# Another order of work in a polysketch attention and mixture-of-experts attention kernel

## The chip, the cores and the metric

The kernel runs on one core of a Trainium2 chip. The metric is the time of one execution on the device in microseconds (us). The engines are named as in the profile: PE (TensorE, matmuls; PEld its weight loads), DVE (VectorE), ACT (ScalarE), POOL (GpSimd) and SP (SyncE, which issues most of the DMAs). Each engine carries out its own instructions in the order in which the program issues them, and waits on semaphores for what other engines and DMAs have to deliver.

## The reference

A linear attention over four batches of four heads is followed by an attention of four experts, of which each row of the sequence uses two.

```python
def phi(x):                       # q, k, v: (4, 4, 1088, 32); S1, S2: (8, 32)
    a = np.einsum('rd,bhsd->bhsr', S1, x)
    b = np.einsum('rd,bhsd->bhsr', S2, x)
    return np.einsum('bhsi,bhsj->bhsij', a, b).reshape(*x.shape[:-1], 64)
q_p, k_p = phi(q), phi(k)
kv  = np.einsum('bhsf,bhsd->bhfd', k_p, v)
num = np.einsum('bhsf,bhfd->bhsd', q_p, kv)
den = np.einsum('bhsf,bhf->bhs', q_p, k_p.sum(2))[..., None] + 1e-06
x = (num / den).transpose(0, 2, 1, 3).reshape(4, 1088, 128)

topk, w = ...                     # the 2 best of 4 logits x @ w_gate, softmax over the 2
for e in range(4):
    q, k, v = x @ wq[e], x @ wk[e], x @ wv[e]          # 128 -> 64
    a = causal_softmax(q @ k.T / 8)
    ye = a @ v @ wo[e]
    for kk in range(2):
        out += (topk[:, :, kk] == e)[..., None] * w[:, :, kk:kk+1] * ye
```

The output has the shape (4, 1088, 128), in f32.

## The kernel before

**Work and tiles.** The loop over the four batches (batch, L1285) writes down the same jobs for each. First the polysketch attention: k, q and v are loaded by halves or quarters and turned by DVE; PE makes the two sketches of each (job "sketch", L524); DVE turns them back ("back", L527); DVE or POOL multiplies them into 64 features ("features", L529 to L532); PE sums the features with v ("sums") and divides for x. Batch 0 does it by rows (attend_rows, L603), the batches 1 to 3 turned (attend_turned, L696), which are prepared while the batch ahead of them runs its experts. Then choose_experts (L811) makes the gate: logits on PE, some twenty small DVE instructions, and masks that go through DRAM.

The experts' attention works on 17 tiles of 64 rows a batch; as each row has two chosen experts a tile fills 128 partitions. The tiles come in three groups, (0,6), (6,12) and (12,17) (L141). For each group queries (L1011) makes the queries of all experts and picks the chosen ones with a predicated copy (L1031). For each tile scores (L1045) makes a chain over all engines: score on PE (L1056), take with mask and maximum on DVE (L1068), exp on ACT (L1084), guard on ACT or POOL (L1090, L1092), invert on DVE (L1095), weigh on POOL (L1099), turn A on DVE (L1104). values (L1114) then multiplies with x on PE (L1132), sorts the sums by expert (L1162 to L1175: keep, patch, spread and scale V), and outputs (L1201) projects with the folded weights Mo, copies out of PSUM and stores. The last group of the last batch has its own end (L1219 to L1242): three pieces of 128 rows, each with a copy "keep out 3.0.x" by ACT or DVE (L1238) and a store "store out 3.0.x" by SP or ACT (L1241).

**The order of the work.** Nothing is scheduled by the compiler. job (L78) only notes a job: its name, the engine or the two engines that can do it, what it reads and makes, and the buffers that it holds. The list ORDER (L22) then names all 1287 jobs by number, and Plan.run (L84) issues them in this order. A letter behind a number picks the engine: a is the first of the job's two, b the second; for a dummy b means that it is left out. A job's figures of time, landing and rank in the code were used in making the list and do nothing in the kernel. Buffers are handed out from queues of free ones in the order of the list, so the list also sets which earlier job a buffer's next user waits for. PSUM has four pairs of banks (the pool "ps"), SBUF has three query buffers "qs", three of masks "mb", six of working tiles "w", two of each of "AT", "agg" and "ob".

```python
n, a = (int(word[:-1]), "ab".index(word[-1])) if word[-1] in "ab" else (int(word), 0)
j = self.jobs[n]
if j["eng"][a] != "-":
    for h in j["holds"]:
        if h not in self.where:
            self.where[h] = free[h[0]].popleft()
    j["f"](j["eng"][a])
```

**The jobs that the text speaks of**, by their numbers. 2 and 3: loads of S1 and S2, by SP and ACT. 4: "table" (L247), a first activation, with which ACT loads its table. 5 to 44: dummies (L250), each of two matmuls of 128x512 in bf16 on a buffer of zeros; the result isn't used. 52: load of the weights w0 by SP. 60 and 63: pick8 and onehot, small constants. 74 and 75: load k0.0 by SP and k0.1 by ACT (L429). 76 and 77: load q0.0 by SP and q0.1 by ACT. 78 to 81: loads of v0 by SP. 95: features k0.2, by POOL or DVE. 106: keep sums 0.0 and 109: keep qf 0.0, copies out of PSUM by ACT or DVE (L194 is the one copy helper). 177 and 219: reciprocals of the gate's shares (L906). 402 and 403: turn k1.0 and k1.1 on DVE (L490). 406 to 408: sketch k1 and its two back transposes. 385: out 0.2, the projection of batch 0's last group (L1210). 557 and 558: score and take of tile 1.7. 1126 and 1130: scale V 3.0.x, by POOL or DVE. 1135, 1137, 1139: keep out 3.0.0, 3.0.1 and 3.0.2; 1136, 1138, 1140: their stores.

Of the kernel before, what the change touches and what calls it, by code (L numbers as in the profile page):

```python
# [27 lines left out]
205 173 430 223 245 189 249a 166a 190a 693 699 250a 421 215 436 206 207 431 211a 194 216 318 195 432a 691 212 251 319  # L28
217 160 433a 134 322a 434 161a 247 196 213 248 224 29b 252 698 703 437 197a 438a 191 214 439a 690 704 192 267 268 706a
705 225a 420 323a 193 198 218a 199 219 422 269 324 220 695a 275 276 71 145 320 73 709a 696a 72 277 440 137 423 321 990  # L30
325 278 221 291 270 200 260 707a 279a 226 292 141 708a 261 293 711a 177 262 710a 263a 280 271a 441 443b 227 283 228 442a
284 178a 281 34b 285 272 286 282 253 991 713 461 294 136 326 327 712 462 254 714a 255 229 264 702 287a 273 265 328 256a
230 231 295b 463 465 994 715 464 716 296 30b 989 144 11b 288 140 266 274 701 721 466 289 329 330b 138 233a 722a 297 335
290 257 358 235b 234a 232a 237 258 236 331 298 334 43b 359 361 351 467 350 31b 360 336 471 362 363 238 342 337 352 239
343 723 476 344 338b 332 259 477 468 345 353 346b 478 725 472 354a 724 333 479 444 364b 139 347 339 18b 28b 299 300 480b
448 301 302 365 726 340 481b 482 447 303 304 305a 341 483 348 445 306a 719 349 307b 366 519 241 240 985 520 308a 505 446
473 474 143 310 309 732 242 367 311 987 512 506 355 142 733 243a 312 543 14b 986 356 513 727 491 514 542 734 357 498 521
515b 492 314 507 717 315 499 735a 313 544 469 728 316a 522b 36b 41b 545 730b 736a 5b 516 500 501b 368 737 718 523 546a
493 997 475a 547b 548 369 244 370 452 371 494a 549 372 373 517 374 729b 375 376 377a 450 524 996 502 525 484 731 518 495
988 508b 378b 380b 588 589 485 509 720 15b 503 381 455 379a 486 382 35b 487b 510 550 496 590 591 511 384 497 738 504 551  # L40
565 592a 453 740a 739a 564 566 572 573 488 383 580 489 574 490 581 992a 451 582 1000 575 758 460 576a 44b 449 454 1002
616 577 615 1004b 552 1001 993b 567 759 760 470 618 619a 617 1008b 620a 593 594 761 526 527 528 12b 553a 621 622 1003a
578 37b 554 529a 530a 1007a 555 568b 579 531a 534 385 33b 1005b 763 583 639 1006a 532a 569 386 584a 570 640 533 623 456
764 317 585 571 648 457 556 557 586 535 641 624 595 647 536 642 558 765 1010 458 649 762 625 587 1009 632 559 560b 631
774 655 650 16b 626 627a 561 633 773 562 656 1011a 651a 995 634 538 776 652 628 653 563 657 635b 778a 658 629 777b 779
636 388 659 643b 775 780 539 537 644 768 1012 637 802 630 803 660 795 796 540a 769 654 661a 816 817 797 645 1018 596 770
597 662 646 19b 663 1013 1019b 598 781 39b 818 664 788 599 771 804 459 805b 782 600 789 601 638 806 798a 783 741 790 389
999 742 799 998 665 604a 603b 744 666 602a 606 605a 667 745 607 668 743 772a 1020 609 746 608 766 387 1022 38b 669 784b
1021 670 785 23b 786 840 787 809 26b 751 1023 1024 839 791a 1029 1030 807 843b 844a 671 1025 1017 672 1027a 810 673 792
819b 676a 675a 800 845 677a 841 811 541 1031 674b 679 749 842 820 846 1032a 40b 611 610 755 678 808 1026a 1028 747 1033a  # L50
847 612 821 812a 1016 21b 862 848 1014 1034 748 801 1015 681 813 885 680 861 613a 886 822 887 849 814 1035 793 863 854
767 1036b 794 877 878 815 850a 855 24b 869 879 870 888 913 912 864 865b 1037a 916a 753 856 866 871 1055 823 857a 757 824
917b 1056 825 858 867 918 915 851 1057 880 872 914 889b 1058 890 390 881b 827a 882 682 883 873a 831 1059 874 919 884
1060 891 859 826a 830 868 828a 860 952 953 852 683 754 853 936 833 27b 937 929 928 829a 875 954 955 892 938 930 956 920
921 957 832 944 931 1065 939 922 945 1061 750 958b 940b 1063 1141 1144 946 1142 959 1143 923 876 893 960 941 1146a 1066
947 894 614 1038 924b 756 942 1145b 948b 925 1147 895 752 896 897 949 898 943 961 1067 1148 899a 687 902a 901b 835 932a
900a 1042 904 926 20b 1039 903 950 834 1172 1171 1041 905 933 1040 836 1149 1156 951 837a 1173 906 1068 1150 1188 934
927 1187 1180 1174 1175b 935 1189 1157 1179 1163 1190 684 1164 1215 1165 1158 686 1069a 13b 1166 1181 1151 1217 1214
1167b 1182 1216 1159b 1176 962 1219b 1218b 1064 963 964 1168 1177 965 1183a 966 1045 838 1191a 1220 1221 1169 967 968
1152a 1178 1153 1160 1184 969 970 971a 974a 1170 1222 1192 973b 975 1185 1193 1194 1223 1246 972a 976 977 1247 1257 1255  # L60
1048 1154 1224 1225 1248 1186 1254 6b 978 1256 1071 1070 1161 1162 1231 1258 1044 1249 1062 1230 1232 1075a 1226b 685
1250b 1155 1227 1239 1228 1238 1050 907 1047 1074b 1259 1046 1076 1072 1260b 1233 908 1251 1234b 1073 909 1252 979 1240
1077 1241 910a 1235 1043 1106 1261 1229 1236 1085 1242b 980 1262 1107 1086 1049 1237 1108 1109a 1253 911 1099 1243 1051
1110 1113 1195 1111 1114 982 1196 1053 1263 984 1100 1087 981 1197 1115 1198 1101 1078 1088b 1244 1245 1092 1054 983
1116a 1199 1200 1079 1089 1093 1102a 1094 1264 1052 1090 1201a 1265 1266 1267 1268 1202a 1095b 1204b 1206 1080 1269
1081a 1270 1203b 1207 1205 1091 1271 1096 1082 1272 1097 1083 1208 1103 1084 1211 1104 1117 1118 1276a 1210 1098 1119
# [1283 lines left out]
```

## Time and profile before

| | us |
|---|---|
| runs | 264.88, 262.51, 262.26 |
| their median | 262.51 |
| the profiled execution | 260.8 |
| its span, from its first to its last record | 259.0 |
| busy in it: PE, DVE, POOL, ACT | 249.3, 210.4, 158.4, 105.3 |
| granted clock of PE, mean | 0.997 |

The profile is of one execution, and its times count from the span's start. A row of a timeline gives the start, the duration, the engine, the line, the operation with its tiles (out<-in, partitions x elements, type) and how many instructions the row takes together (x); in square brackets, where the engine was idle before it, how long, and what it waited for. "ACTq" and "SPq" are the queues in which ACT and SP issue DMAs. "L1132" is line 1132 of the kernel.

### The profile page before, as it was taken

Reading aid. Unit: us, or ns where it says so; the run is one execution under the profiler, and the core shown is the slowest. Engines: PE = TensorE matmul, PEld = TensorE weight load, DVE = VectorE, ACT = ScalarE, POOL = GpSimd, SP = SyncE. Lnnn points to the kernel's source line nnn. Section 1 sums busy time; section 2 is a strip of 40 time slices with the busy share of each in tenths; the row PEclk is TensorE's granted clock in tenths of the full one; section 3 lists DMA queues with packets and bytes.
Section 4 is the critical chain, followed back from the end, with each engine's and each line's share of the span. In section 5 each row is a group of like instructions: output and inputs, shape, how many; then the busy total and the mean of one; then the engine's idle time right before and its main releaser. Section 6 shows DMA issues by size and latency. Waiting matters only on the chain.

```text
span 259.0 us, 9930 instructions
## 1 busy us (share of the span) xinstructions
PE 249.3 (96%) x4158; PEld 185.1 (71%) x4159; DVE 210.4 (81%) x532; ACT 105.3 (41%) x276; POOL 158.4 (61%) x271
## 2 busy tenths in 40 slices
PE   8798988999999999999999999999999999999994
PEld 3477554566498896665789786765896975789984
DVE  6998999999988787989998389899979649794342
ACT  2354446762704407634643034623525317243220
POOL 4867589948488816196762798283683633733640
PEclk9999999999999999999999999999999999999998
DMA  6953489505359445304403671404442226440012
GB/s 217 239 147 94 133 231 202 114 11 112 121 82 254 119 127 144 109 3 112 112 3 47 135 215 58 134 3 146 107 66 76 61 66 184 121 110 3 3 34 56
DMA packets 40381, 27.88 MB, mean 108 GB/s; under 512 B 25872, under 2 KB 35600, under 8 KB 40336
## 3 DMA queue, kind: packets, MB, share of 16 engines
q1 hardware_dynamic: 39744, 26.56, 42.0%
q8 instruction: 32, 0.52, 0.9%
q10 hardware_dynamic: 592, 0.69, 0.7%
q14 instruction: 13, 0.11, 0.2%
HBM read 22.62 MB, written 4.62 MB: 105 GB/s over the span
## 4 chain that ended last, share of the span: by engine, by line
PE 83%; POOL 7%; DVE 4%; DMA 3%; issue 2%; ACTq 1%; ACT 0%; SPq 0%; POOLq 0%; DVEq 0%
PE pair L1132 30%; PE pair L1056 26%; PE pair L1018 9%; PE pair L1260 7%; POOL fp L532 4%; PE pair L1210 3%; DMA in<-in_k_dram 2%; PE pair L771 2%; PE pair L576 1%; PE pair L524 1%; PE pair L1236 1%; DVE w L527 1%; PE pair L822 1%; POOL w L548 1%; DMA md<-cT 1%
## 5 line engine op out<-in xcount | busy, mean ns | idle before, releaser
L1099 POOL TENSOR_SCALAR w<-w,rs,sh 128x192 f32<-128x192 f32 (+14 forms) x68 | 55.9, 827 | 32.9 <-DVE rs L1095 31.4
L1056 PE MATMUL pair<-xT,qs 128*128 128x384 f32 (+11 forms) x216 | 73.6, 478 | 1.9 <-DVE rs L1095 1.0
L1084 ACT ACTIVATE w<-w,mx 128x192 f32<-128x192 f32 (+16 forms) x68 | 52.5, 773 | 50.1 <-DVE mx L1068 44.8
L1056 PEld LDWEIGHTS pair<-xT,qs 128*128 128x128 f32 x216 | 38.3, 190 | 28.5 <-issue 11.9
L1104 DVE STREAM_TRANSPOSE AT<-w 128x128 f32<-128x128 f32 (+14 forms) x68 | 50.7, 759 | 6.2 <-POOL w L1099 6.0
L1068 DVE CUSTOM_DVE_ANT_0 w<-pair,mask 128x896 f32<-128x896 f32 (+15 forms) x68 | 48.2, 724 | 4.4 <-PE pair L1056 3.5
L1166 POOL TENSOR_TENSOR agg<-agg,mb 128x768 f32<-128x768 f32 (+1 forms) x22 | 34.0, 1560 | 18.6 <-issue 8.7
L1132 PEld LDWEIGHTS pair<-AT,xra 32*128 32x128 f32 x1136 | 41.6, 185 | 3.7 <-DVE AT L1104 1.1
L1132 PE MATMUL pair<-AT,xra 32*128 32x160 f32 (+5 forms) x1136 | 44.1, 302 | 0.0
L194 ACT COPY agg<-pair 128x384 f32<-128x384 f32 (+1 forms) x36 | 15.0, 467 | 52.3 <-PE pair L1132 47.8
L1018 PE MATMUL pair<-xT,Mq 128*128 128x384 f32 (+1 forms) x96 | 34.3, 479 | 0.0
L532 POOL TENSOR_TENSOR fp<-w 128x576 f32<-128x576 f32 x22 | 27.1, 1250 | 1.3 <-DVE w L527 0.6
L1132 PE MATMUL pair<-AT,xrb 32*128 32x160 f32 (+5 forms) x752 | 27.3, 287 | 0.0
L1132 PEld LDWEIGHTS pair<-AT,xrb 32*128 32x128 f32 x752 | 26.4, 185 | 0.8 <-issue 0.7
L1031 DVE COPY_PREDICATED qs<-mb,pair 128x768 f32<-128x768 uint16 (+1 forms) x24 | 23.2, 967 | 1.8 <-DMA mb<-me 0.8
L1018 PEld LDWEIGHTS pair<-xT,Mq 128*128 128x128 f32 x96 | 17.0, 190 | 9.5 <-DVE mx L1068 1.1
L1092 POOL TENSOR_SCALAR rs<-zs 128x1 f32<-128x1 f32 x34 | 8.2, 242 | 23.8 <-ACT w L1084 21.9
L1260 PEld LDWEIGHTS pair<-Mo,agg 128*128 128x128 f32 x168 | 20.6, 192 | 2.7 <-issue 0.8
L1260 PE MATMUL pair<-Mo,agg 128*128 128x128 f32 x168 | 21.1, 276 | 0.0
L527 DVE STREAM_TRANSPOSE w<-pair 128x576 f32<-128x576 f32 x16 | 11.8, 760 | 3.9 <-PE pair L524 3.7
L194 DVE COPY agg<-pair 128x384 f32<-128x384 f32 (+1 forms) x10 | 5.1, 523 | 11.5 <-ACT agg L194 10.6
L1162 DVE COPY_PREDICATED agg<-mb,pair 128x384 f32<-128x384 uint16 (+1 forms) x24 | 12.6, 548 | 2.0 <-ACT agg L194 2.0
(173 smaller groups left out, 290.4 us busy)
## 6 DMA issues: line engine op xcount, KB each, us to landing
xra<-xd SPq DMA_DIRECT2D x16, 192.0 KB, 3.9
xrb<-xd SPq DMA_DIRECT2D x16, 192.0 KB, 4.7
xrc<-xd SPq DMA_DIRECT2D x16, 160.0 KB, 3.9
in<-in_k_dram SPq DMA_DIRECT2D x7, 272.0 KB, 4.3
mb<-me SPq DMA_DIRECT2D x3, 576.0 KB, 4.2
mb<-me SPq DMA_DIRECT2D x6, 288.0 KB, 5.6
in<-in_q_dram SPq DMA_DIRECT2D x3, 544.0 KB, 5.2
xd<-w SPq DMA_DIRECT2D x12, 136.0 KB, 3.6
```

What stands on the lines that cost most here:

```text
L194: (nc.scalar.copy if eng == "ACT" else VEC[eng].tensor_copy)(o, i)
L532: VEC[e].tensor_tensor(out=f, in0=a[:, :, None, R : 2 * R].to_broadcast([128, NJ, R, R]), in1=a[:, :, 0:R, None].to_broadcast([128, NJ, R, ...
L1018: nc.tensor.matmul(plan[ps[x]][:, y, 0:w], Mq[:, ((1, 2), (0, 3))[x][y]], plan[xT][:, 64 * t0 : 64 * t1], start=True, stop=True)
L1031: nc.vector.copy_predicated(chosen(), c, rows(plan[ps[x]]))
L1056: nc.tensor.matmul(plan[p][:, y, 0 : c1 - c0], plan[qs][:, 128 * t : 128 * t + 128], plan[xT][:, c0:c1], start=True, stop=True)
L1068: nc.vector.tensor_tensor_reduce(out=o, in0=src, in1=msk, scale=-1.0, scalar=mx[:, b, i, x - 1 : x] if x else 3e38, op0=ALU.add, op1=ALU.m ...
L1084: nc.scalar.activation(out=a, in_=a, func=ACTF.Exp, bias=mx[:, b, i, last : last + 1], scale=-1.0, accum_out=zs[:, b, i : i + 1])
L1099: nc.gpsimd.tensor_scalar(out=a, in0=a, scalar1=rs[:, b, i : i + 1], scalar2=plan[("sh", b)][:, i : i + 1], op0=ALU.mult, op1=ALU.mult)
L1104: nc.vector.transpose(dst[:, 0 : keys // 32, t], plan[A][:, 0:keys].rearrange("p (j s) -> p j s", s=32))
L1132: nc.tensor.matmul(plan[Vk[g // 2]][:, g % 2, lo : 32 * nt], plan[(f"xr{j // 12}", b)][rows, j % 12], a[rows, j, lo:], start=(j == 0), sto ...
L1166: nc.gpsimd.tensor_tensor(out=a, in0=a, in1=masks_in(plan[mb], w)[:, 2 * x : 2 * x + 2], op=ALU.mult)
L1260: nc.tensor.matmul(plan[p][0:m, 0, 128 * x : 128 * x + 128], plan[agg][:, e, 128 * x : 128 * x + m], Mo[:, e], start=(e == 0), stop=(e == ...
```

## The change

Only the list ORDER is changed, in all of its lines. It names the same 1287 jobs; some 72 of them have another letter, and so another engine: among them copies out of PSUM (L194), about thirty guards (L1090, L1092), the features k0.2 (95), the scale V 3.0.x (1126, 1130). The dummy 13 (18) is carried out in the new list and left out in the old one, so eight dummies run in place of seven. The order within each engine differs nearly everywhere. At the start, ACT's table (4) is ahead of load k0.1 (75), and pick8 (60) is POOL's first piece of work. Out 0.2 (385) comes ahead of score and take 1.7.0 (557, 558) in the old list and behind them in the new one. At the end, keep out 3.0.1 (1137) is on DVE and its store (1138) on SP; in the old list both were ACT's.

The first lines of both lists, the lines with the jobs named above, and the last:

```diff
 ORDER = """
-400 1 0 22a 2 3 84 76 48 45 77 49 74 42a 46 9a 51 88 10a 75 52 4 85 50 89 17a 86 87 78 81 401 47 97 90 98 79 100a 80 7a
-54 58 53 397 66 59 99 64 25a 391 82a 102a 65 56 92 395 91 392 101b 83a 103b 394 67a 95b 110 96a 60 94a 93a 403 111a 396
-402 112 114 115a 113a 108 109b 105 57 104 107b 106b 406 116 63a 122 399a 408 407 117a 126 55 398a 118 68 123 70 127 69
-61 128 124 410a 119 393 413a 414b 62a 692 133 409a 120 129a 411a 121b 405 416 412a 125a 415 404 697 146 417a 148 147 154
-130 149 152 162 163 179 418 180 150 132 424 153 184a 155 156 425a 151 689 183a 131 158 169 174 182 157a 167 159a 168 688
-181 170 185 426 164 694 171 186 700 427 201 208 419 202 135 175 428 176 203 187 222 204a 209 188 172 429 246 435 165 210
...
-325 278 221 291 270 200 260 707a 279a 226 292 141 708a 261 293 711a 177 262 710a 263a 280 271a 441 443b 227 283 228 442a
...
-578 37b 554 529a 530a 1007a 555 568b 579 531a 534 385 33b 1005b 763 583 639 1006a 532a 569 386 584a 570 640 533 623 456
...
-32b 1273a 1274a 1209 1112 1277 1275a 1105 1120 1278 1121 8b 1122 1212a 1128 1123a 1125 1280 1279 1213 1127a 1281 1124
-1126b 1131 1129 1132 1133 1282 1130b 1134 1135b 1284 1139a 1286 1285 1283 1140b 1136a 1137a 1138b
+1 3 0 2 48 76 77 4 74 51 37b 75 10a 60 46 52 84 50 81 54 49 88 8a 45 89 7a 17a 85 22a 78 80 97 86 79 53 87 400 98 100a
+397 90 55 99 91 92 63b 83a 64 391 102a 47 101b 96a 392 66 103b 24a 19a 59 82a 65 67a 401 114 115a 396 39b 108 95a 94a
+110 111a 93a 403 56 109a 112 113a 105 104 106a 394 116 58 402 406 107b 57 122 408 407 123 395 410a 117a 68 126 118 69
+413a 409a 127 119 399a 61 128 120 398a 393 70 414b 124 129a 412a 405 416 121b 125a 411a 62a 415 404 146 147 152 688 148
+154 417a 693 162 418 163 153 149 179 180 183a 155 150 424 425a 156 158 151 167 184a 131 168 181 157a 170 130 689 169
+159a 185 419 182 426 186 201 700 164 9b 174 215 175 427 133 202 208 132 165 428 203 209 176 216 204a 171 429 205 430 246
+222 245 166a 435 210 211a 223 436 217 187 206 694 172 431 207 433a 177 212 250a 691 194 432a 18a 249a 195 137 318 160
...
+569 453 621 768 579 1006a 528 529a 585 557 622 553a 530a 32b 531a 1005b 558 760 623 33b 593 624 317 625 586 533 761 385
...
+1104 1098 1105 982 1211 1278 1275b 1120 984 1121 1276a 1122 1123a 1277 1128 1279 1125 1280 1281 1126a 1212a 1127a 1213
+1124 1131 1132 1133 1129 1282 1284 1283 1130a 1134 1139a 1285 1135b 1286 1140b 1136a 1137b 1138a
 """.split()
```

More of the change, by code (lines that the diff above doesn't have):

```diff
@@ new lines @@
+413a 409a 127 119 399a 61 128 120 398a 393 70 414b 124 129a 412a 405 416 121b 125a 411a 62a 415 404 146 147 152 688 148
+154 417a 693 162 418 163 153 149 179 180 183a 155 150 424 425a 156 158 151 167 184a 131 168 181 157a 170 130 689 169
+159a 185 419 182 426 186 201 700 164 9b 174 215 175 427 133 202 208 132 165 428 203 209 176 216 204a 171 429 205 430 246
+222 245 166a 435 210 211a 223 436 217 187 206 694 172 431 207 433a 177 212 250a 691 194 432a 18a 249a 195 137 318 160
+173 218a 188 319 247 699 697 437 189 219 213 196 248 161a 251 690 438a 197a 434 252 439a 323a 322a 190a 703 421 422 191
@@ new lines @@
+224 192 692 220 268 214 704 420 705 193 423 706a 267 71 698 134 72 269 276 707a 275 440 710a 73 277 135 270 324 320 225b
+221 198 321 271b 708a 199 226 292 227 272 291 325 23b 278 695a 696a 293 200 178a 273 441 145 442a 31b 253 136 702 228
+274 283 711a 443a 254 701 294 279a 28b 284 709a 260 326 280 327 295a 261 285 461 296 462 262 712 255 328 329 713 281
+714a 229 230 330b 231 715 256a 297 263b 721 463 286 282 464 233b 466 235a 257 264 359 258 465 358 722a 471 716 298 140
+234a 351 265 360 232a 141 237 236 259 238 266 350 989 334 335 467 287a 139 352 720 985 472 361 138 342 343 239 362 16b
@@ new lines @@
+331 723 468 288 336 344 353 289 363 332 991 290 476 479 337 724 345 477 725 333 364a 354b 355 480a 481b 726 478 356 365
+299 14b 300 301 302 303 304 338a 482 483 143 241 346a 306a 366 339 340 732 990 444 142 367 448 307a 305a 718 341 473 347
+447 445 733 505 446 474 308b 240 242 348 309 311 310 727 512 986 728 506 519 243b 994 312 513 545 520 514 349 498 499
+515a 988 357 544 521 144 314 729a 491 516 996 313 38b 315 469 507 543 15b 542 734 992b 316a 546a 997 492 508b 475a 493
+735a 494a 20b 517 368 26b 522a 736a 369 509 370 495 500 993a 371 372 451 719 547b 501b 29b 548 523 717 373 524 510 374
@@ new lines @@
+375 518 450 449 737 376 730b 484 731 549 525 377a 496 379a 502 503 244 378b 497 380a 485 383 589 588 486 550 382 381 738
+452 511 11b 590 551 572 573 740a 564 574 384 487a 504 739a 565 488 575 576a 580 581 566 1000 489 582 758 615 490 591 577
+1002 1004b 616 470 583 618 759 552 459 617 567 1001 526 568a 619a 578 1008a 592a 620a 584b 527 987 25b 762 1007b 1003a
+569 453 621 768 579 1006a 528 529a 585 557 622 553a 530a 32b 531a 1005b 558 760 623 33b 593 624 317 625 586 533 761 385
+1010 534 570 559 386 763 594 1009 626 1011a 627a 536 769 764 532b 554 535 587 648 1012 647 571 560a 639 628 640 649 595
@@ new lines @@
+765 774 999 629 631 561 630 562 458 641 632 460 773 778a 656 642 655 455 555 776 775 633 538 657 770 777a 643a 1013 563
+634 995 650 658 644 779 651a 780 539 659 556 537 771 635b 540a 795 802 796 645 456 636 41b 387 652 653 660 454 1014 661a
+803 637 646 662 816 1018 596 663 654 597 817 1019b 598 599 998 664 781 457 638 788 782 789 818 600 601 741 790 665 772a
+804 819a 12b 602b 797 745 603b 744 791b 604a 820 541 792 605a 666 805b 607 821 742 608 806 667 606 1020 609 390 822 807
+668 783 1017 1021 1022 40b 743 669 388 1023 670 766 1024 27b 1029 751 839 809 810 840 784b 1025 671 672 1030 43b 673 747
@@ new lines @@
+785 1026a 844a 808 748 841 843a 1027a 1031 1028 793 675a 786 842 1016 811 787 798b 676a 845 812a 612 677a 1015 1033a
+1032a 749 846 389 13b 674a 794 756 813 678 679 611 799 800 854 885 1034 855 610 613a 750 35b 886 887 861 862 888 847 863
+848 814 681 864 1035 1037b 815 878 801 680 856 877 870 869 849 34b 754 889b 857a 746 879 850a 913 912 871 1036a 1055 823
+824 916b 872 1056 865b 1057 1058 890 851 1059 825 873a 6b 1065 917b 866 767 880 914 829a 1066 757 827a 915 918 752 858
+828a 867 826a 881b 868 859 682 852 891 919 882 929 1060 830 853 928 937 874 892 875 831 936 883 1061 945 683 833 930 884
@@ new lines @@
+931 938 832 920 876 932b 921 753 953 614 922 860 21b 944 946 952 939 1063 947 1142 923 954 1141 1067 955 933 948a 1146a
+1143 956 1144 893 949 1145a 686 1038 934 957 958a 894 940a 1039 1147 1148 959 960 895 935 896 897 898 901a 1172 1171 755
+924b 950 900a 925 961 1041 42b 941 951 904 834 899a 835 926 1164 1163 902a 44b 927 1173 905 903 1040 1187 1042 1165 1149
+1150 1188 1156 1189 36b 942 836 1190 906 1174 1191b 1215 943 1068 684 837b 1069a 687 1180 1151 1157 1158 1179 1192 1217
+1181 1214 1159b 1216 962 1064 1182 963 1219b 1183b 964 1152b 965 1166 1044 1175a 1193 838 966 1160 1153 1167b 967 1184
@@ new lines @@
+1218a 1161 1220 1194 968 1185 969 1221 970 1168 1176 1222 1162 685 972a 973a 976 1255 971b 974a 1045 1154 1254 977 975
+978 1177 1223 1155 1256 1257 1258 1230 1224 1178 1259 1047 1247 1225 1231 1246 1169 1071 1052 1046 1070 1248 1062 1186
+907 1260a 1073 5b 1051 1232 1226b 1075a 1072 1043 1261 1262 909 1048 1074b 1238 1227 1249 908 1170 1076 1228 1050 1233
+1077 1239 1106 1234a 910a 1240 1235 1229 1085 979 1236 1086 1107 911 1241 1250a 980 1242b 1251 1243 1108 1244 1245 1263
+1113 1099 1195 1109a 1049 1252 1196 1100 1114 30b 1197 1087 1088a 1253 1198 1237 1078 1092 1054 1093 1115 1094 1079 1199
@@ L69 @@
+1200 1201b 1095b 1264 1096 1080 1265 1205 1266 1267 1204b 1116b 1110 1081b 1268 1053 1089 1117 1269 1082 983 1083 1202b
+1090 1101 1203b 1111 1207 1091 1084 1270 1206 1208 981 1102a 1271 1103 1272 1118 1209 1112 1119 1210 1097 1273a 1274a
+1104 1098 1105 982 1211 1278 1275b 1120 984 1121 1276a 1122 1123a 1277 1128 1279 1125 1280 1281 1126a 1212a 1127a 1213
+1124 1131 1132 1133 1129 1282 1284 1283 1130a 1134 1139a 1285 1135b 1286 1140b 1136a 1137b 1138a
 """.split()
```

37 lines of the change are left out of this document (removed).

## The prediction

> **What bounds the kernel now.** I read the page first: busy time by engine, then the 40 slices, then the chain that ended last. The slices show where TensorE (PE) is not full, and the chain's shares show what it was waiting on there.
>
> ```profile
> PE 249.3 (96%) x4158; PEld 185.1 (71%) x4159; DVE 210.4 (81%) x532; ACT 105.3 (41%) x276; POOL 158.4 (61%) x271
> PE   8798988999999999999999999999999999999994
> PE 83%; POOL 7%; DVE 4%; DMA 3%; issue 2%; ACTq 1%; ACT 0%; SPq 0%; POOLq 0%; DVEq 0%
> ```
>
> PE is the bound: 96% busy and 83% of the chain. It is under 9 only in the first slices and in the last one. The second view is the table of windows, cut where PE first runs without gaps (42.12) and where DVE's last copy is nearly over (255.60). Columns: the stretch, its length, then busy us of PE, PEld, DVE, ACT and POOL with counts, PE's clock, the DMA share, GB/s.
>
> ```profile
> 0.00:42.12 42.12, 36.00 (x758) 22.45 (x759) 37.16 (x111) 19.39 (x54) 30.00 (x76) 1.00 0.71 178
> 42.12:255.60 213.48, 213.30 (x3400) 162.67 (x3400) 173.21 (x422) 85.41 (x221) 128.42 (x196) 1.00 0.39 94
> 255.60:259.00 3.40, 0.00 (x0) 0.00 (x0) 0.03 (x1) 0.53 (x2) 0.00 (x0) 0.80 0.28 71
> 5.40:15.40 10.00, 8.50 (x200) 5.93 (x202) 9.26 (x13) 3.92 (x7) 8.98 (x20) 1.00 1.03 226
> 26.00:42.10 16.10, 13.94 (x168) 7.74 (x164) 15.44 (x60) 8.96 (x31) 11.80 (x33) 1.00 0.76 184
> ```
>
> So the time has three parts. In 213.48 us PE is idle for 0.18: no order can shorten it while PE's work is the same, it can only put stalls in. In the first 42.12 PE is idle for 6.12 and part of its busy time is dummies; there DVE is the bound (9.26 of 10.00, 15.44 of 16.10). The tail of 3.40 has no PE at all. A new order can gain at the start and in the tail, and lose anywhere.
>
> The sum is made against the profiled run, 260.8 us: a span of 259.0 and 1.8 around it. The median of the runs is 262.51, 1.71 above; I add the sum's change to the median.
>
> **The change, part by part.** Both lists hold the same 1287 jobs. About 72 words take another engine. PE has one job more (an eighth dummy) and one change of mode fewer (68 to 67).
>
> *Tail.* Timeline of the last stretch (start, duration, engine, line, instruction, idle before and releaser):
>
> ```profile
> 253.38 0.52 DVE L1175 TENSOR_TENSOR agg<-agg,mb 128x384 f32<-128x384 f32 x1
> 253.49 1.82 SPq L1216 DMA_DIRECT2D out_dram<-ob  x4
> 255.34 0.29 DVE L194 COPY ob<-pair 128x128 f32<-128x128 f32 x1 [1.44 <-PE pair L1236]
> 255.61 0.27 ACT L194 COPY ob<-pair 128x128 f32<-128x128 f32 x1 [3.37 <-PE pair L1236]
> 255.66 0.36 SPq L1242 DMA_DIRECT2D out_dram<-ob  x1
> 256.30 0.27 ACT L194 COPY ob<-pair 128x128 f32<-128x128 f32 x1 [0.42 <-ACT ob L194]
> 256.60 0.35 ACTq L1242 DMA_DIRECT2D out_dram<-ob  x1
> ```
>
> ACT copies piece 2, issues its store, and only then copies piece 1 and issues that: last issue at 256.60. In the new list piece 1 is DVE's (1137b), right behind piece 0, and its store is SP's (1138a). DVE's copies end at 255.34+0.29 = 255.63 and about 255.63+0.29 = 255.92. The store goes out when copy and SP allow: the copy-to-issue gap is 0.03 (255.63 to 255.66), so 255.95 by the copy; SP's own pitch is 1.82/4 = 0.455, so 255.66+0.455 = 256.12 by the queue. That is 256.60-256.12 = 0.48 earlier; I take -0.5. The ends: 256.60-255.95 = -0.65, and 0 if SP's second store is held as long as ACT's was. The landing behind the last issue is 1.6 either way by the row below.
>
> ```profile
> out_dram<-ob ACTq DMA_DIRECT2D x2, 64.0 KB, 1.6
> ```
>
> *The load of k0.1.* On ACT's queue it stood ahead of the activation table (75 before 4); now it stands behind (4 before 75). Two views: ACT's timeline, and the DMA issues (KB each, then median us from issue to landing).
>
> ```profile
> 1.82 0.44 ACTq L429 DMA_DIRECT2D in<-in_k_dram  x1
> 2.29 1.28 ACT L247 ACT_TABLE_LOAD   x1 [2.29 <-issue]
> 3.59 0.20 ACT L247 ACTIVATE warm<-warm 128x1 f32<-128x1 f32 x1
> ```
>
> ```profile
> in<-in_q_dram SPq DMA_DIRECT2D x1, 272.0 KB, 3.3
> in<-in_q_dram ACTq DMA_DIRECT2D x1, 272.0 KB, 3.8
> in<-in_k_dram ACTq DMA_DIRECT2D x1, 272.0 KB, 5.1
> AT<-in_moe_wq_dram SPq DMA_DIRECT2D x1, 128.0 KB, 5.6
> ```
>
> The issue goes from 1.82 to 1.82+1.28+0.20 = 3.30, if the queue waits for the table; if it issues beside it, nothing is lost. The load landed at 6.93 (1.82+5.1). Issued at 3.30 it lands between 6.60 (3.3 later, not late) and 8.90 (5.6 later, +2.0). I take 4.0 after the issue, near the 3.8 of the other load on this queue: 7.30, +0.4. DVE is behind it, then PE's sketches and the whole of k0.
>
> The Trainium skill speaks to both halves of this. "DMA: Bandwidth & Descriptors", section "Queues, rings and completion order", says that each DMA engine takes turns, packet by packet, between the queues that have work; the durations above (3.3 to 5.6) grow with what was issued before and fit one line as well as turns, but by that rule k0.1 would not stand behind all that SP issues in between, the +2.0 would be out and the sum stays as it is. "ScalarE: Activation LUTs", section "What ACT_TABLE_LOAD costs", adds a drain of about 1.38 us to a load of 1.28; this trace has the 1.28, but the activation starts 0.02 behind it, so a drain is not seen. By that rule the load would be 0.4+1.38 late and, less what is absorbed below (0.5), the sum would be an estimate of 263.2 instead of 261.9: the place and the sign of rival A.
>
> *DVE up to 18 us.*
>
> ```profile
> 12.09 1.50 DVE L532 TENSOR_TENSOR fp<-w 128x576 f32<-128x576 f32 x1
> ...
> 13.52 1.42 DVE L532 TENSOR_TENSOR fp<-w 128x576 f32<-128x576 f32 x2
> 15.37 1.37 DVE L490 STREAM_TRANSPOSE in<-in 128x544 f32<-128x544 f32 x2 [0.43 <-DMA in<-in_k_dram]
> 16.66 0.65 DVE L194 COPY fp<-pair 128x512 f32<-128x512 f32 x1
> 17.34 0.46 DVE L194 COPY kvz<-pair 64x66 f32<-64x66 f32 x2
> 17.93 1.45 DVE L527 STREAM_TRANSPOSE w<-pair 128x576 f32<-128x576 f32 x2
> 11.81 1.17 POOL L532 TENSOR_TENSOR fp<-w 128x576 f32<-128x576 f32 x1
> 16.88 0.78 PE L524 MATMUL pair<-in,SKk 32*32 32x288 f32 x32 [0.55 <-ACT vp L194]
> 18.80 0.82 POOL L548 TENSOR_TENSOR w<-w 128x288 f32<-128x288 f32 x1 [2.00 <-DVE w L527]
> ```
>
> The product of features k0.2 moves from POOL to DVE: 1.42/2 = +0.71. DVE's product of 12.09 lasts 1.50 beside POOL's of 11.81 to 12.98; with POOL's gone I take 0.71 for it too, -0.79 (ends: 0, if POOL is not what slows it, and -0.79). Balance -0.08; with the +0.4 DVE is done at 13.52+1.42-0.08+0.4 = 15.26, still ahead of the load of k1.1 for which it waits to 15.37. So the late load is absorbed up to 15.37-14.86 = 0.5. From 15.37 on DVE loses the copy of 0.65 and one of the two of 0.46/2 to ACT: -0.88. Of this 0.25 counts (17.93 to 17.68), since the transpose behind needs PE's sketch of k1, over at 16.88+0.78 = 17.66. ACT takes them in a wait of 6.3 for v:
>
> ```profile
> ACT vp L194 <- DMA w<-in_v_dram: 6.3, 1, 6.3
> ```
>
> pick8 goes to the front of POOL, onehot to ACT: nothing, as POOL idles 2.00 ahead of 18.80; were that used up, it would cost its 2 us of POOL work less that idle.
>
> *26 to 42 us.* Two reciprocals (219 and 177) move forward into this stretch. The row of 35.41 is of the same kind: two by 0.20. DVE waits 0.25 in the row of 39.79. Net +0.15.
>
> ```profile
> 35.41 0.20 DVE L906 RECIPROCAL ch<-ch 128x6 f32<-128x6 f32 x1
> 39.79 1.38 DVE L749 STREAM_TRANSPOSE fp<-fp 128x1152 f32<-128x1152 f32 x1 [0.25 <-POOL fp L532]
> 1.25 4.21 PE L251 MATMUL pair<-idle 128*128 128x512 bf16 x10 [1.25 <-DVE idle L244]
> 42.12 1.81 PE L1056 MATMUL pair<-xT,qs 128*128 128x288 f32 x5 [1.02 <-DVE rs L1095]
> ```
>
> The eighth dummy (18a) is two matmuls of 4.21/10 = 0.42: 0.84, in front of query 0.2.0. It lies in PE's idle 6.12, of which 1.02 is just ahead of 42.12: nothing, and up to 0.84 if that wait is gone. PE full: 42.12-0.25+0.15, that is 0.1 earlier.
>
> *From 42 us on.* The same work on PE; one mode change fewer is under one matmul's 0.42, taken as 0. Copies that change engine there stand beside a full PE: 0, unless PE waits for one (rival B). The two scale V 3.0.x go to POOL at the end. Like the sum of 253.38 they have 384 columns, so 0.52 each on DVE and, by the ratio of the products above (1.17 to 0.71), some 0.86 on POOL: 0.34 slower each. DVE, freed of both, and POOL work side by side there: 0; without that cover the last output, and the end, would be up to 0.7 later.
>
> **Sum:** -0.1 (start) + 0 (middle) - 0.5 (tail) = -0.6: 260.8 to 260.2 for a profiled run, 262.51 to 261.9 for the median.
>
> **The rivals.** *A, k0.1 lands late (+2.0).* Its load queues behind SP's loads, or the table holds the issue longer. For it: the DMA share is 1.03 in 5.4 to 15.4. Against it: 0.5 is absorbed at 15.37. The start is then 2.0-0.5-0.1 = +1.4, with the tail +0.9: 263.4. Within 1%.
>
> *B, slower: PE stalls for its four psum pairs.* A PE job takes a pair that a DVE job frees, and DVE's queue has a new order. It is tightest at out 0.2 (385). The new list has score and take 1.7.0 (557, 558) ahead of it, the old one behind, and hands it the pair which that take frees. DVE's first and last of the 13 jobs in question, and PE's row up to out 0.2:
>
> ```profile
> 105.52 0.78 DVE L527 STREAM_TRANSPOSE w<-pair 128x576 f32<-128x576 f32 x1
> 111.44 2.39 PE L1210 MATMUL pair<-agg,Mo 128*128 128x320 f32 x8
> 119.90 0.65 DVE L1068 CUSTOM_DVE_ANT_0 w<-pair,mask 128x512 f32<-128x512 f32 x1
> ```
>
> In the old order that take ended at 119.90+0.65 = 120.55; the new one, with PE's work ahead of out 0.2, needs it by 111.44+2.39 = 113.8. DVE's 13 jobs from 105.52 up to and with it sum to 8.44 by their durations, so 113.96: 0.2 late. I find four more such places (sums 3.1, scores 2.6, 3.7 and 3.15.01 of the later batches). The point from which it decides is 2.6+0.6 = 3.2 us of stalls, some 0.65 at each of five places: then 265.2 and more. For it: DVE has 173.21 of 213.48 there, so 81%, and no long slack. Against: 40 us of DVE's idle time lie in that stretch, and a stall is paid once, not at each place anew, as DVE catches up.
>
> *C, faster by over 1%.* The start shortens by 2.1 more because POOL's lead of 2 us and the removed copies reach 42 us: 259.8. For it: PE idles 6.12 there. Against: DVE is 15.44 of 16.10 busy in 26 to 42, with the same work in it.
>
> *D, the spread copy brings nothing.* SP's second store starts as late as ACT's did, or its landing is longer: 262.4.
>
> **How the numbers follow.** About 1% (2.6 us) is what a measurement of this kernel can tell from no change. Forecast 0.46; A 0.14; B 0.20; C 0.08; D 0.12. Forecast, A and D are within 1%, together 0.72; B is slower, 0.20; C is faster, 0.08. The range reaches from 260.2 (the forecast with another 1.7 of the start's 6.12 idle) to 265.2 (B's threshold) and leaves out C and the most of B; the likeliest case's own range is 261.2 to 262.6.
>
> **What would show it.** Right: the last two stores are issued at about 256.1 less the start's shift, one on SP; k0.1's transpose on DVE starts near 7.3; the feature products on DVE near 12 us are all about 0.75; PE is full from about 42.0 and idle under 0.3 behind. Wrong: that transpose starts past 8.5 (A); PE idle over 2 us after 42, with DVE's takes (L1068) as releasers (B); PE full before 40.5 (C); the last issue at 256.6 (D).

## The result, and the profile after

Over 20 runs of each kernel the changed one took 259.88 us (median, 259.2 to 262.07) and the one before 262.74 us (260.6 to 265.9). The ratio is 0.9918 with a 95% interval of 0.9892 to 0.9943, so -2.15 us (-1.5 to -2.8), and a later set of 12 runs gave 0.9933 (0.9901 to 0.9965). These two medians are of all 20 runs; every ratio, and the medians and counts further down, leave out the slow executions, at a granted clock of 0.991 to 0.994. The forecast was 261.9 us and "within 1%"; the kernel is faster by 0.8%, 1.5 us more than the forecast gain of 0.6.

The first thing to see is that the two profiled executions do not show this. The profiled one of after took 260.19 us (span 258.5), the profiled one of before 260.8 (259.0): a difference of 0.6, just the forecast, which had been worked out on that one execution. That agreement is luck, as the three stretches show. The lines of the page, and the windows cut at the same events as those of before (PE full, PE's last matmul):

```profile
PE 249.4 (96%) x4159; PEld 185.6 (72%) x4161; DVE 207.2 (80%) x527; ACT 108.0 (42%) x287; POOL 157.8 (61%) x265
PE   7888998999999999999999999999999999999995
```

```profile
0.00:42.45 42.45, 36.48 (x760) 22.54 (x762) 36.33 (x112) 21.43 (x55) 27.27 (x73) 1.00 0.69 180
42.45:255.37 212.92, 212.89 (x3400) 163.08 (x3400) 170.59 (x415) 86.31 (x231) 130.51 (x193) 1.00 0.40 94
255.37:258.50 3.13, 0.00 (x0) 0.00 (x0) 0.30 (x2) 0.27 (x1) 0.00 (x0) 1.00 0.31 77
```

Cut at PE's end, 255.53, the row of before is:

```profile
42.12:255.53 213.41, 213.30 (x3400) 162.67 (x3400) 173.14 (x422) 85.41 (x221) 128.42 (x196) 1.00 0.39 94
255.53:259.00 3.47, 0.00 (x0) 0.00 (x0) 0.10 (x1) 0.53 (x2) 0.00 (x0) 0.81 0.29 72
```

The start is 0.33 longer (forecast 0.1 shorter), the middle 0.49 shorter (forecast the same), the tail 0.34 shorter (forecast 0.5). The missing 1.5 us were looked for in executions that no profile had shown: the kernel before was profiled again, and both orders were taken apart.

### The profile page after: what moved, and what is told of

Its sections match the earlier page's. It is cut to its first block, busy times and chain, and to the rows that moved or that the text cites. A ratio compares the mean times of both kernels' runs of the same rounds, so it can differ in the third digit from the quotient of the medians.

```text
span 258.5 us, 9931 instructions
## 1 busy us (share of the span) xinstructions
PE 249.4 (96%) x4159; PEld 185.6 (72%) x4161; DVE 207.2 (80%) x527; ACT 108.0 (42%) x287; POOL 157.8 (61%) x265
## 4 chain that ended last, share of the span: by engine, by line
PE 83%; DMA 6%; DVE 5%; POOL 2%; issue 2%; ACTq 0%; ACT 0%; DVEq 0%; POOLq 0%
PE pair L1132 30%; PE pair L1056 26%; PE pair L1018 9%; PE pair L1260 7%; PE pair L1210 3%; DMA wgr<-in_moe_w_gate_dram 2%; DMA w<-in_v_dram 2%; PE pair L771 2%; POOL fp L532 2%; DMA in<-in_q_dram 2%; PE pair L524 1%; PE pair L576 1%; DVE qs L1031 1%; PE pair L1236 1%; PE pair L822 1%
## 5 line engine op out<-in xcount | busy, mean ns | idle before, releaser
L1099 POOL TENSOR_SCALAR w<-w,rs,sh 128x960 f32<-128x960 f32 (+15 forms) x68 | 56.5, 837 | 32.1 <-DVE rs L1095 29.5
L1056 PE MATMUL pair<-xT,qs 128*128 128x320 f32 (+11 forms) x216 | 73.7, 478 | 1.3 <-DVE rs L1095 0.7
L1084 ACT ACTIVATE w<-w,mx 128x768 f32<-128x768 f32 (+16 forms) x68 | 52.3, 769 | 48.0 <-DVE mx L1068 44.3
L1068 DVE CUSTOM_DVE_ANT_0 w<-pair,mask 128x192 f32<-128x192 f32 (+14 forms) x68 | 48.3, 723 | 11.3 <-PE pair L1056 9.1
L1104 DVE STREAM_TRANSPOSE AT<-w 128x64 f32<-128x64 f32 (+15 forms) x68 | 50.7, 758 | 4.6 <-POOL w L1099 4.5
L194 ACT COPY agg<-pair 128x384 f32<-128x384 f32 (+1 forms) x34 | 14.1, 464 | 48.4 <-PE pair L1132 45.5
L1031 DVE COPY_PREDICATED qs<-mb,pair 128x768 f32<-128x768 uint16 (+1 forms) x24 | 23.1, 964 | 2.6 <-DMA mb<-me 1.2
L1092 POOL TENSOR_SCALAR rs<-zs 128x1 f32<-128x1 f32 x28 | 6.3, 226 | 20.8 <-ACT w L1084 17.9
L194 ACT COPY qs<-pair 128x384 f32<-128x384 f32 (+1 forms) x18 | 7.8, 459 | 16.4 <-PE pair L1018 16.4
L527 DVE STREAM_TRANSPOSE w<-pair 128x576 f32<-128x576 f32 x16 | 11.6, 755 | 3.2 <-PE pair L524 3.0
```

What stands on the lines that cost most here:

```text
L194: (nc.scalar.copy if eng == "ACT" else VEC[eng].tensor_copy)(o, i)
L1031: nc.vector.copy_predicated(chosen(), c, rows(plan[ps[x]]))
L1056: nc.tensor.matmul(plan[p][:, y, 0 : c1 - c0], plan[qs][:, 128 * t : 128 * t + 128], plan[xT][:, c0:c1], start=True, stop=True)
L1068: nc.vector.tensor_tensor_reduce(out=o, in0=src, in1=msk, scale=-1.0, scalar=mx[:, b, i, x - 1 : x] if x else 3e38, op0=ALU.add, op1=ALU.m ...
L1084: nc.scalar.activation(out=a, in_=a, func=ACTF.Exp, bias=mx[:, b, i, last : last + 1], scale=-1.0, accum_out=zs[:, b, i : i + 1])
L1099: nc.gpsimd.tensor_scalar(out=a, in0=a, scalar1=rs[:, b, i : i + 1], scalar2=plan[("sh", b)][:, i : i + 1], op0=ALU.mult, op1=ALU.mult)
```

## The experiments

Two theories stood against each other at first. "Late loads": an engine's queue stands behind a load that lands late in some executions, at the start. "Full stretch": the loss of before lies behind 42 us, where its profile had no idle PE.

**The kernel before, again** (no edit).

> The kernel before, unchanged, for a second profile beside the runs of the kernel before. The change measured 0.9918, but the two profiled executions differ by 0.6 us only, and the profiled execution of before (260.8) lies at the lower end of its 20 runs (260.6 to 265.9). All theories expect a ratio of 1.000 +- 0.003. Theory 'late loads' (the old order loses 1 to 5 us in some executions because a load lands later than in the profiled one and an engine's queue stands behind it): a profile that is over 262 us shows PE idle for more than the 6.1 us of the first profile, with a DMA or work that hangs on one ahead of it, in the first 45 us. Theory 'full stretch' (the loss is where PE is full): such a profile has the same first 42 us and a longer stretch behind, by PE's idle time or by its clock (0.997 in the first profile).

Measured: 0.9963 (0.9922 to 1.0003) for the same code, so a ratio no further from 1 than this shows little by itself. The profiled execution took 261.83 us. Its windows:

```profile
0.00:41.92 41.92, 36.63 (x759) 22.57 (x759) 37.27 (x111) 19.32 (x54) 29.99 (x76) 1.00 0.70 180
41.92:256.58 214.66, 213.25 (x3400) 162.35 (x3400) 172.52 (x422) 85.28 (x221) 128.32 (x196) 1.00 0.38 94
```

The start is no longer than in the first profile; the middle is 1.25 longer with the same busy time. PE's and DVE's timelines near 154 us and SP's ahead of them show where:

```profile
151.62 1.56 PE L1018 MATMUL pair<-xT,Mq 128*128 128x384 f32 x4
154.47 1.80 PE L1260 MATMUL pair<-Mo,agg 128*128 128x128 f32 x14 [1.30 <-DVE qs L1031]
```

```profile
151.37 0.16 DVE L1095 RECIPROCAL rs<-rs 128x1 f32<-128x1 f32 x1
153.32 1.01 DVE L1031 COPY_PREDICATED qs<-mb,pair 128x768 f32<-128x768 uint16 x1 [1.78 <-DMA mb<-me]
```

```profile
146.15 0.31 SPq L800 DMA_DIRECT2D xra<-xd  x1
146.56 0.84 SPq L947 DMA_DIRECT2D mb<-me  x2
```

PE waits 1.30 us to begin out 1.1.1, because the psum pair for it is freed by pick 2.1.0 (L1031) of the next batch, and that pick waits 1.78 us for its masks. The masks' fetch (766) was issued at 146.56, right behind fetch x 2.00 (746), which itself waits for the stores of x to land. The chain that ended last has them in a row: the last store of x (from 141.49, 4.58 us), the masks (from 146.97, 6.22), the pick. By the times the same landing, at 146.07, also holds back q3, the transposes at L527 ahead of the pick on DVE, which wait 5.03 us to 146.20. In the first profile the same three came at 145.07, 145.49 and 151.58, and PE went on without a gap:

```profile
145.07 0.31 SPq L800 DMA_DIRECT2D xra<-xd  x1
145.49 0.84 SPq L947 DMA_DIRECT2D mb<-me  x2
```

```profile
151.58 1.02 DVE L1031 COPY_PREDICATED qs<-mb,pair 128x768 f32<-128x768 uint16 x1 [0.79 <-DMA mb<-me]
```

```profile
153.50 1.95 PE L1260 MATMUL pair<-Mo,agg 128*128 128x128 f32 x16
```

So it is "late loads", but in the full stretch, and only in a part of the executions.

**The old list with the new tail** (`1137a` to `1137b`, `1138b` to `1138a`).

> The old list with only the copy of piece 1 on DVE and its store on SP (1137b, 1138a). By the two profiles the time from PE's last matmul to the end of the span is 3.47 before and 3.13 after: every theory expects 0.9987 (-0.3 us), the forecast 0.998 (-0.5), and no more than that; if the tail alone gave 0.993 or less, the other theories fall.

Measured: 0.9986 (0.995 to 1.0022), and 3.13 us from PE's end to the end of the span (258.07 to 261.2), as in after. The tail is worth 0.34 to 0.4. This profile has the stall at 154 us too, and a second one near 49 us:

```profile
155.97 2.02 PE L1260 MATMUL pair<-Mo,agg 128*128 128x128 f32 x16 [1.40 <-DVE qs L1031]
```

```profile
48.70 0.67 PE L771 MATMUL pair<-fp,kvr 32*32 32x288 f32 x6
49.99 1.51 PE L771 MATMUL pair<-fp,kvr 32*32 32x256 f32 x58 [0.62 <-DMA kvr<-kd]
```

There the last repeat sums (423) stands on SP behind two fetches of x; in the new list it is ahead of them.

**New start, old rest; and old start, new rest.** A first pair took the first 260 words of one list and then all other jobs as the other has them.

> The first 260 words of the new list (up to about 45 us), then all other jobs in the order of the old list, with its letters. Theory 'late loads': the gain is here, 0.993 to 0.995 (-1.3 to -1.8 us), with a narrower spread of the runs. Theory 'full stretch': 1.000. The profile of one execution may hardly differ from that of before, whichever holds.

> The first 260 words of the old list, then all other jobs in the order of the new list, with its letters (so with the new tail). Theory 'late loads': 0.9987 (the tail's -0.3 us). Theory 'full stretch': 0.992 to 0.994 (-1.6 to -2.1 us).

Measured: 1.0026 (0.9994 to 1.0059) and 0.9965 (0.9932 to 0.9997). Both were spoilt: dummies of the second list that the first one leaves out ran at 45 us, two in the one and four in the other, in the middle of the full stretch:

```profile
45.19 1.90 PE L251 MATMUL pair<-idle 128*128 128x512 bf16 x8
```

Less these 1.90 the second would be near 0.989, an estimate; that suggested that the gain is not in the start alone. The pair without these dummies comes last.

**One word moved in the old list: masks first.**

```diff
-... 772a 1020 609 746 608 766 387 1022 ...
+... 772a 1020 609 608 766 746 387 1022 ...
```

> The old list with one word moved on SP: fetch masks 2.1 (766) is issued ahead of fetch x 2.00 (746), which waits for the stores of x to land. In two of three profiles of the old order PE stood idle 1.3 to 1.4 us at 154 us, in out 1.1.1, which takes the psum pair of pick 2.1.0 (L1031), which waited 1.8 to 1.9 us for these masks. Theory 'late masks' (a large part of the gain is this stall, in the executions that have it): no PE idle over 0.3 us near 154, pick 2.1.0 starts without a DMA wait over 0.8, and a ratio of 0.995 to 0.998 (-0.5 to -1.3 us). Rival 'letters' (keep V 1.2.2 on DVE instead of ACT, or DVE's order, makes the stall): the stall stays, 1.000. Rival 'spread' (the gain is many small things): 0.999 to 1.000.

Measured: 0.9958 (0.9934 to 0.9982), -1.1 us, with all runs within 260.43 to 261.67. That is hardly further from 1 than the same code above, so the size is not firm. The stall is absent in the profiled execution, as it was in the first profile of the old order; SP, DVE and PE:

```profile
144.93 0.82 SPq L947 DMA_DIRECT2D mb<-me  x2
146.39 0.32 SPq L800 DMA_DIRECT2D xra<-xd  x1
```

```profile
151.84 1.03 DVE L1031 COPY_PREDICATED qs<-mb,pair 128x768 f32<-128x768 uint16 x1
```

```profile
153.29 1.95 PE L1260 MATMUL pair<-Mo,agg 128*128 128x128 f32 x16
```

The pick has no idle time ahead of it. The rival "letters" falls, as keep V 1.2.2 is still on DVE. The pick, and not that copy, frees the pair that out 1.1.1 takes. Here back q3 waited 5.00 us for a store of x, as in the stalled execution, and the masks were there in time all the same. One profile does not show that the stall is gone from every execution.

**The old list with three edits**: masks first, `423` ahead of `145`, and the new tail.

> The old list with three edits: masks first as in the run above; repeat sums 1.3 (423) ahead of fetch x 0.23 (145), since one profile of the old order had PE idle 0.6 and a matmul group 1.2 us longer near 49 us behind that load; and the new tail. Theory 'late loads on SP's queue': this has nearly the whole gain, 0.992 to 0.995 (-1.3 to -2.1 us), and no PE idle over 0.3 after 45 us. Rival 'spread': 0.997 to 0.999, the tail's 0.3 us and little else.

Measured: 0.9957 (0.993 to 0.9984), median 260.52 against 260.81 of the one edit in the same set, and no idle time of PE over 0.3 behind 45 us. Beside it ran the new list at 259.98 and the kernel before at 261.88: by the medians the three edits have 1.4 of its 1.9 us. The 0.992 to 0.995 of "late loads" was missed, and so was the 0.997 to 0.999 of "spread"; by the ratio the second and third edit add nothing to the first that can be told.

**The same word moved back in the new list: x first.**

```diff
-... 1023 670 766 1024 ... 746 ...
+... 1023 670 746 766 1024 ...
```

> The new list with one word moved: fetch x 2.00 (746) stands directly ahead of fetch masks 2.1 (766) on SP, as in the old list, and waits there for the last store of x (issued at 145.2 in the profile, some 3 to 4 us to land). Theory 'late masks': the masks are issued near 148.5 instead of 146.6, pick 2.1.0 waits over 1.5 us for them, PE is idle 1 to 2.5 us near 154, and the kernel is 1 to 2.5 us slower than the new one (0.996 to 1.002 against before). Rivals: as the new list, 0.992.

Measured: 0.9978 (0.9941 to 1.0015), median 261.48, 1.5 us over the new list beside it. The masks went out at 145.94 and not at 148.5, since the store of x had left earlier in this execution. 2.19 us of waiting for masks on DVE and then an idle PE came as forecast:

```profile
152.14 2.13 DVE L1031 COPY_PREDICATED qs<-mb,pair 128x768 f32<-128x768 uint16 x2 [2.19 <-DMA mb<-me]
```

```profile
153.29 2.02 PE L1260 MATMUL pair<-Mo,agg 128*128 128x128 f32 x16 [1.55 <-DVE qs L1031]
```

But this does not show the moved word as the cause. The masks landed at 152.0, and at 151.9 in the first profile of the new list, which had no stall; here PE was full at 41.28 and not at 42.45, so it was at out 1.1.1 earlier. The next run has the stall without the move.

**The new list, again** (no edit).

> The changed kernel, unchanged, for a second profile and for the size of the gain on this chip. 0.992 +- 0.003. Theory 'late loads on SP's queue': no PE idle over 0.3 us after 45 us in this profile either.

Measured: 0.9933. The expectation on the profile was wrong: the new order has the stall as well, in this execution (260.8 us).

```profile
152.71 2.14 DVE L1031 COPY_PREDICATED qs<-mb,pair 128x768 f32<-128x768 uint16 x2 [2.07 <-ACT agg L194]
```

```profile
153.86 2.02 PE L1260 MATMUL pair<-Mo,agg 128*128 128x128 f32 x16 [1.43 <-DVE qs L1031]
```

The copy that the row names makes nothing that this pick reads. It was the masks: the second of their two fetches, issued at 145.4, landed 7.2 us later, at 152.6. The view of SP's line L947:

```profile
L947 SPq DMA_DIRECT2D mb<-me x2: 441/518/596, 144.8 to 145.4; - x2
...
DMA to landing us min/median/max: 5.2/6.2/7.2
```

The 12 runs fall into two groups, 258.93 to 259.48 and 260.49 to 261.06, six each; the 20 runs of the result into 13 up to 260.19 and 7 from 260.65. Its two profiled runs lie on the sides where their stall puts them. Of 105 executions of the kernel before, 15 lie at or below 260.8, the time of the first profiled one, which had no stall. So the new order has this stall in some 40% of its executions (13 of 32), the old one by the same reading in most (the median of the 105 is 261.92). Most of these executions have no profile, so the shares are a reading of the times, and a rough one: the profiled execution of the run above took 260.21 with the stall.

**Can it be had in every execution?** Masks first in the new list:

```diff
-... 606 1020 609 390 822 ... 743 669 388 1023 670 766 1024 ...
+... 606 1020 609 766 390 822 ... 743 669 388 1023 670 1024 ...
```

> The new list with one word moved on SP: fetch masks 2.1 (766) directly behind spread V 1.1.1 (609), ahead of repeat sums 3.3, the last store of x of batch 2 and two stores of the output. In the second profile of the new order PE stood idle 1.43 us near 154, behind pick 2.1.0, as in the old order; its masks were issued at 144.8 and came at 152.7. Theory 'late masks' (in both orders a part of the executions has this stall, and fetches of x issued beside the masks make them late): the masks are issued 1.5 to 2.5 us earlier, no PE idle over 0.3 us after 45 us, runs of narrower spread, 0.989 to 0.992 against before (-0.3 to -0.7 us against the new order). Rival 'not the masks': the stall can still appear, 0.992 to 0.993.

Measured: 0.9974 (0.9949 to 1.0), median 260.8 beside 261.79 for the kernel before, where the new list had 259.98 beside 261.88: worse, not better. The runs stand close together (260.56 to 261.65), as if nearly all had the stall. DVE and PE:

```profile
149.98 0.49 DVE L1068 CUSTOM_DVE_ANT_0 w<-pair,mask 128x320 f32<-128x320 f32 x1 [4.79 <-DMA xd<-w]
...
152.67 2.10 DVE L1031 COPY_PREDICATED qs<-mb,pair 128x768 f32<-128x768 uint16 x2
```

```profile
153.79 2.02 PE L1260 MATMUL pair<-Mo,agg 128*128 128x128 f32 x16 [1.52 <-DVE qs L1031]
```

The masks, issued at 143.07, no longer hold the pick. But store x 2.1 now went out at 145.27, behind them, and take 2.4.0 writes into the working tile that this store frees. It began at 149.98 in place of 147.88, and the pick behind it on DVE was as late as ever. Hence a last attempt, the store and then the masks (`... 609 743 766 390 ...`):

> The new list with two words moved on SP: behind spread V 1.1.1 (609) come store x 2.1 (743) and then fetch masks 2.1 (766), ahead of the two stores of the output and repeat sums 3.3. With the masks alone moved, the store of x went out at 145.3 and landed at 149.9, and the take of tile 2.4 (L1068), which writes into the buffer that this store frees, waited 4.8 us; pick 2.1.0 behind it on DVE came at 152.7 as before, and PE stood idle 1.5 us. Theory 'one queue, two waits' (at this place DVE needs both the store of x landed by about 147.9 and the masks by about 151.6, and SP's order decides which is late): the store is issued near 142.5 and the masks by 144.5, the take starts with its score near 147.9, pick 2.1.0 near 151, and no PE idle over 0.3 us after 45 us; 0.988 to 0.991 against before (-0.4 to -1.0 us against the new order). Rival 'it is neither' (the place has a third wait, or the two DMAs beside each other are both late): an idle of PE near 154 again, 0.993 to 0.997.

Measured: 0.997 (0.9949 to 0.9992). The rival was right, there is a third wait:

```profile
146.12 1.45 DVE L527 STREAM_TRANSPOSE w<-pair 128x576 f32<-128x576 f32 x2 [5.02 <-DMA xd<-w]
...
152.10 1.38 DVE L749 STREAM_TRANSPOSE fp<-fp 128x1152 f32<-128x1152 f32 x1 [2.24 <-POOL fp L532]
...
153.53 2.11 DVE L1031 COPY_PREDICATED qs<-mb,pair 128x768 f32<-128x768 uint16 x2
```

Back q3 also needs a tile from a store of x, and waits 5.02 us for it; the features on POOL and a transpose then come late, and PE idles 1.64 ahead of out 1.1.1. This third wait is the one that the old order had in its second profile (5.03). No version beats the new list.

**The start, without stray dummies.**

> The first 260 words of the old list (to about 45 us), the rest in the order of the run above, with no dummies in that rest. It is the earlier run with the old start again, which by its profile carried four dummies (1.90 us) at 45 us. Theory 'the start gives nothing': equal to the run above within 0.3 us, 0.988 to 0.992. Theory 'the start gives' (or the eighth dummy costs): over 0.5 us of difference, either way.

> The first 260 words of the new list, the rest in the order of the old one, with no dummies in that rest (the earlier run of this kind carried two dummies there). Theory 'the start gives nothing': 0.998 to 1.001, with the same stalls as before behind pick 2.1.0 in a part of the executions; the load of repeat sums 1.3 is within the new start, so that one place of the old order is mended, up to -0.3 us. Theory 'the start gives': 0.995 or less.

Measured: 0.9974 (0.9951 to 0.9997), the same as the run with the new start; and 0.995 (0.9921 to 0.9979), the value of "the start gives" and not the 0.998 or more of "the start gives nothing". So ahead of the new rest with masks first the new start gives nothing, and ahead of the old rest it gives some 1.3 us, with the repeat sums moved and a stall at 154 us of 0.84 in place of 1.3 to 1.4. A start that shifts DVE's queue against the stores may change how long that stall is, and then the two parts do not add, but that is argued from one profile; how much belongs to the start alone stays open.

## Why the prediction was right where it was, and where not

The forecast was made from a median of 262.51 us; 0.9918 of that is 260.36, inside the stated range (260.2 to 265.2) by 0.16, and under 1%. The likeliest case's own range, 261.2 to 262.6, was missed. That the wider one held is luck: its lower end was made of idle time of the start, and the time came from the middle. The size was off by 1.5 us, and nearly all of it by one term of the sum, the middle. The interval of the ratio also shows that a change of under 1% can be told from none here.

- *"From 42 us on: 0"* failed. It was read from one execution, in which pick 2.1.0 waited 0.79 us for its masks and ended 0.90 us ahead of out 1.1.1 (152.60 to 153.50). That row of DVE was in the trace: 0.79 us of waiting on a DMA by an instruction that holds PE's next psum pair. A landing some 1 us later makes it a stall. The gain from having it in 40% of the executions and not in most is 1.3 to 1.4 by some 0.45, about 0.6 us (an estimate from the counts above).
- The same term missed a steady part. PE's busy time between its first full matmul and its last is 213.30 and 213.25 in two profiles of the old order and 212.89 and 212.45 in two of the new, with 3400 matmuls each: 0.4 to 0.85 less, where I had counted one change of mode and put it at 0, and had held that no order can shorten a stretch without idle time. The second profile of the new list:

```profile
42.06:255.97 213.91, 212.45 (x3400) 162.78 (x3400) 170.55 (x415) 86.21 (x231) 130.02 (x193) 1.00 0.39 93
```

  All twelve profiles without stray dummies agree: 213.09 to 213.86 in six with the old rest, 212.45 to 213.23 in six with the new one, medians 213.28 and 212.59, so 0.7 less. It goes with the rest and not with the start: 212.65 with the old start and the new rest, 213.09 the other way. What makes it wasn't tried apart; PE's timeline shows the old order with more and shorter groups between 44 and 56 us, but that it is these is argued, not shown.
- *Tail, -0.5*: measured -0.34 by the windows of the two first profiles, and 3.08 to 3.14 us in all nine profiles with the new tail against 3.47 to 3.57 in the five with the old one, so about -0.4. The last issue came where it was worked out, at 255.50+0.83-0.36 = 255.97 and so 0.60 behind PE's end (forecast 256.12-255.53 = 0.59); DVE's second copy and SP's second store are there:

```profile
255.18 0.49 DVE L194 COPY ob<-pair 128x128 f32<-128x128 f32 x2 [1.94 <-PE pair L1236]
255.45 0.27 ACT L194 COPY ob<-pair 128x128 f32<-128x128 f32 x1 [3.37 <-PE pair L1236]
255.50 0.83 SPq L1242 DMA_DIRECT2D out_dram<-ob  x2
```

  The rest is the way from the last issue to the end of the span, which I had kept the same: 2.53 in place of 2.40.
- *Together*: 0.6 for the stall, 0.7 for PE's busy time and 0.4 for the tail are 1.7 of the 2.15 us, within its interval of 1.5 to 2.8. The first of them is an estimate; what the rest is stays open.
- *The load of k0.1*: right in time by luck (its transpose at 7.20, forecast 7.3), wrong in cause. ACT's queue issued it at 1.87, beside the table load, and not behind it; it landed 5.3 us later and not 4.0 (before: 5.1).

```profile
1.80 1.28 ACT L247 ACT_TABLE_LOAD   x1 [1.80 <-issue]
1.87 0.38 ACTq L429 DMA_DIRECT2D in<-in_k_dram  x1
3.09 0.20 ACT L247 ACTIVATE warm<-warm 128x1 f32<-128x1 f32 x1
```

  Rival A fell with that, and the rule of turns between queues that spoke against it was not tested, as the issue hardly moved. So did the drain that the Trainium skill ("ScalarE: Activation LUTs", section "What ACT_TABLE_LOAD costs") puts behind the table load of a switch to a different set: here, at the program's first load, the activation starts 0.01 us behind it, as before it had 0.02.
- *DVE up to 18 us*: the products were right, five in 3.73 us, so 0.75 each, with none at 1.50. The term behind them failed: I left the landing of k1.1 where it was. SP issued this load at 9.41, ahead of the 9.74 of before, but DVE waited for it to 16.16, not to 15.37: 6.75 us behind the issue in place of 5.63, and 6.6 and 5.4 in the second profiles of the two lists. Why it takes longer in the new list wasn't tried. The back transposes of k1 began at 18.72 and not at 17.68.

```profile
11.35 3.73 DVE L532 TENSOR_TENSOR fp<-w 128x576 f32<-128x576 f32 x5
16.16 1.37 DVE L490 STREAM_TRANSPOSE in<-in 128x544 f32<-128x544 f32 x2 [1.08 <-DMA in<-in_k_dram]
17.56 0.23 DVE L194 COPY kvz<-pair 64x66 f32<-64x66 f32 x1
18.72 1.45 DVE L527 STREAM_TRANSPOSE w<-pair 128x576 f32<-128x576 f32 x2 [0.93 <-PE pair L524]
```

  PE was full at 42.45 and 42.06 in the two profiles of the new list, at 42.12 and 41.92 in those of the old. Over all 14 profiles it was full at 41.28 to 42.45 with the new start and at 41.59 to 42.12 with the old one, means 41.85 and 41.94: the 0.1 of the forecast can't be told from what executions differ by.
- *Rival B* named the right mechanism and the wrong kernel. Out 0.2 did not wait (take 1.7.0 ended at 112.50+0.69 = 113.19, out 0.2 began at 113.70):

```profile
112.50 0.69 DVE L1068 CUSTOM_DVE_ANT_0 w<-pair,mask 128x512 f32<-128x512 f32 x1 [0.39 <-PE pair L1056]
113.70 2.32 PE L1210 MATMUL pair<-agg,Mo 128*128 128x320 f32 x8
```

  PE waits for a psum pair behind a late DVE job in the order before, in two of its three profiles and by the times in most executions, and in the new one in fewer. C and D did not come: not over 1%, and the tail came.

## What to carry to other kernels

An order written out by hand that has no gap in one profile may have one in most executions. Look in the profile for waits of an in-order queue on a DMA that end within a microsecond of where the bound engine would notice, and profile a second execution before putting a stretch at zero. Where several DMAs feed one engine's queue, moving the late one forward on the issuing queue made another late here: list all that this engine needs of that queue before moving one.

## What the runs showed of the hardware

The second of the same two mask fetches landed 5.6 and 6.2 us behind its issue in two executions of the old order, and 4.7 and 7.2 in two of the new. An earlier issue did not mean an earlier start of the pick: in the new order the fetches went out at 146.60 and the pick began at 152.09, and in the other execution at 144.79 and 152.71. A DMA that ACT issues is not held by a table load that ACT is carrying out (1.87, within 1.80 to 3.08).

Where products of 128x576 on DVE and POOL overlap near 10 us, the one that begins later takes longer. On DVE, which takes 0.75 us by itself, it was 1.50 at 12.09 and 0.92 at 9.88, behind products of POOL from 11.81 and 8.45, in the profile before. On POOL, which takes 1.17 when it begins first, it was 1.74 at 8.45 before and 1.68 at 8.76 after, behind products of DVE from 8.40 and 8.64, which kept their 0.76.
